# Reordering one step of a chunked linear-attention recurrence: full-array products in one block, scores in quarter tiles

## The chip, the cores and the metric

The kernel runs on one core of a Trainium2 chip, from inputs in device memory to the output in device memory. The metric is the device time of one execution in microseconds; smaller is better. Engines are named as the profile names them: PE is the matrix engine (PEld its weight loads), DVE the vector engine, ACT the scalar engine, POOL GpSimd, SP the queue that issues most DMAs.

## What is computed

Two layers. The first is a recurrence with a decaying state per batch and head; the second sends each resulting row to one of 16 experts, chosen by a group gate and then an expert gate, and multiplies the expert's output by both gates.

```python
# r, k, v: (4 batches, 8 heads, 768 tokens, 48); w, u: (8, 48)
for t in range(S):
    cur = einsum('bhd,bhe->bhde', u * k_t, v_t)
    y[:, :, t] = einsum('bhd,bhde->bhe', r_t, state + cur)
    state = w * state + einsum('bhd,bhe->bhde', k_t, v_t)
x = y reshaped to (3072 tokens, 384)
g_idx = argmax(x @ w_group);  e_idx = argmax(x @ w_expert[g_idx])
out[token] = g_w * e_w * (relu(x @ w1[g, e]) @ w2[g, e])      # w1: 384x1024, w2: 1024x384
```

## The kernel before

All data is f32. The 3072 tokens are 24 tiles of 128: tile n is the chunk n // 4 of batch n % 4. Tiles 2g and 2g+1 are the group g, and are loaded together. The kernel has two stages: a loop of 24 steps (`for s in range(NT)`) for the recurrence and the routing, and then 16 slots, one expert each.

**One step.** The state is replaced by a product of 128x128 per head: the transposed keys and queries, scaled by powers of w, give the scores; the part after the diagonal is kept, and the diagonal holds r*u*k summed over the head. The functions of a step, with the line that issues the work:

- `values(s)` (L505): the scores' matrix `am` times v, 8 heads, 48 output columns each, into the bank pair `YB`.
- `update(s)` (L516): keys times values, 8 heads, 48x48, into `MS`; `carry(s)` (L529, L530, DVE) adds it to the state R. The last four tiles have none.
- `turn(n, "kT")` and `turn(n, "rT")` (L447): four 128x128 transposes each, both into the bank `TR`; kT is copied out by ACT (L456), rT by DVE with a factor (L458). They work at tile s+3.
- `rows_out(s-1)` (L550, and ACT L554): y back to rows, four transposes into `RW`.
- `scores(s+2)` (L465): 8 heads, 48 rows of contraction, 128x128 each, into `PA`; `mask` (L471, DVE) moves the wanted part to `am`.
- `diagonal(n, e)` (L483, ACT): per head one copy of the identity times the head's sum, in two blocks of four; `sum_own(n)` (L438, DVE) makes those sums from `own` (L421, L423, POOL). `scaled` (L431, POOL) makes the scaled keys that kT is made from. POOL does whole groups (two tiles in one instruction), at even and odd steps.
- `gate_parts(s)` (L540): four products of 32 output columns, into `MS`, copied by ACT to `lT` (L545); `gate_sum(s)` (L564) sums them, into another part of `MS`.
- `state(s+1)` (L496): the state's share of the next tile's y, 8 heads of 48 rows and 48 output columns, into `YB`.
- In every four steps the routing of four finished tiles: `route_1` (DVE, reads `MS`), `route_2`, the prefix products `route_p` (L176, L179), `route_3`, `route_4`, and `route_5` (L215, POOL), which scatters rows to their expert's region `x_sorted`.

**What sets the order.** The schedule is manual: every engine runs its instructions in the order in which the program calls the functions, and waits are put in where a buffer or a PSUM bank is still used. A write of PE into a bank waits for the reads of that bank that stand before it in the program, other columns too. On PE a product is two records in the trace (f32 takes two passes with a weight load each), a transpose is one.

**Forms.** Transposes, `gate_sum` and the prefix use the whole 128x128 array. The values and the update use halves of its columns, the scores halves of its rows, `gate_parts` quarters of its columns, the state quarters (half the rows, half the columns).

Of the kernel before, what the change touches and what calls it, by code (L numbers as in the profile page):

```python
# [13 lines left out]
OP = mybir.AluOpType  # L14
# [13 lines left out]
def kernel(  # L28
# [194 lines left out]
    with ExitStack() as rec:  # L223
# [13 lines left out]
        y_ps = YB[:, :, 0 : 2 * P]  # L237

# [58 lines left out]
        for a in range(2):  # L297
            load_half(raw[0, "k"], k, 0, a, both[a])
            load_half(raw[0, "r"], r, 0, a, both[1 - a])
        zeros = ring.tile([P, XW], FP32, name="zeros")  # L300
# [4 lines left out]
        nc.scalar.dma_start(  # L305
            out=ub.rearrange("p h d -> p (h d)"), in_=bass.AP(tensor=u.tensor, offset=u.offset, ap=[[0, P], [1, H * D]])
        )
# [106 lines left out]
        def own(g, half=None, part=None):  # L414
            rt, kt = raw[g, "r"], raw[g, "k"]
            if g not in dgs:
                dgs[g] = pool.tile([P, 2, H, D], FP32, tag="dg", bufs=3, name="dg")
            dg = dgs[g]
            if half is None:
                if part in (None, 0):  # L420
                    nc.gpsimd.tensor_mul(dg, rt, kt)  # L421
                if part in (None, 1):
                    nc.gpsimd.tensor_mul(dg, dg, spread(ub, 1, 2))  # L423
            else:
                nc.gpsimd.tensor_mul(dg[:, half], rt[:, half], kt[:, half])
                nc.gpsimd.tensor_mul(dg[:, half], dg[:, half], ub)

        def scaled(g, half=None):
            dst = kp[g % NKP][:, :, :, 0:D]
            if half is None:  # L430
                nc.gpsimd.tensor_mul(dst, raw[g, "k"], spread(T2, 1, 2))  # L431
            else:
                nc.gpsimd.tensor_mul(dst[:, half], raw[g, "k"][:, half], T2)
# [8 lines left out]
        def turn(n, name, bank=None, early=False):  # L442
            ps = turned[n, name] = TR if bank is None else bank
            src = (kp if name == "kT" else rp)[(n // 2) % NKP]
            for hc in range(HC):
                two = src[:, n % 2, 2 * hc : 2 * hc + 2, :].rearrange("p e x -> p (e x)")
                nc.tensor.transpose(ps[:, hc, :], two, ident)  # L447
# [3 lines left out]
        def turn_out(n, name):  # L451
# [3 lines left out]
            if name == "kT":  # L455
                nc.scalar.copy(dst, ps)  # L456
            else:
                nc.vector.tensor_tensor(out=dst, in0=ps, in1=pw, op=OP.mult)  # L458

        def scores(n):  # L460
            kT, rT = rkT.pop((n, "kT")), rkT[n, "rT"]
            for hc in range(HC):
                for e in range(2):
                    rows = slice(DP * e, DP * e + D)
                    nc.tensor.matmul(  # L465
                        PA[:, e, P * hc : P * (hc + 1)], lhsT=kT[rows, hc, :], rhs=rT[rows, hc, :],
                        start=True, stop=True, skip_group_check=True,
                    )
# [11 lines left out]
        def diagonal(n, e):  # L480
            du = dus[n].rearrange("p (hc e) -> p e hc", e=2)
            for hc in range(HC):
# [53 lines left out]
        def gate_parts(n):  # L536
            yT = yTs[n]
            for q in range(NQ):
                e, j = q // 2, q % 2
                nc.tensor.matmul(  # L540
                    MS[32 * q : 32 * (q + 1), 0:P], lhsT=gwp[:, 4 * j + e, :], rhs=yT[:, e, j, :],
# [3 lines left out]
            nc.scalar.copy(lT, MS[:, 0:P])  # L545
# [157 lines left out]
        scaled(2)  # L703
        same = ring.tile([P, HC], FP32, name="same")
        LA = 3
        late = []
        left = []
        for s in range(NT):
# [9 lines left out]
            if s % 2 == 0 and g < NG:  # L718
                if g > 2:
                    scaled(g)  # L720
                own(g, None, 0)
            if s % 2 == 1 and g < NG:
                own(g, None, 1)
            for c, i in late[0 : 1 if s < 22 else 2]:
                route_5(c, (i,))
            del late[0 : 1 if s < 22 else 2]
# [8 lines left out]
            if s in (1, 2, 3, 4):  # L735
                fill(s - 1)
            far = s + LA < NT
            values(s)
            update(s)
            values_out(s)  # L740
            for c in range(NB - 1):
                if s == 4 * c + 5:
                    route_e(c)
            carry(s)
# [459 lines left out]
```

## Time and profile before

| | us |
|---|---|
| median of 3 runs | 444.2 (442.93 to 445.17) |
| the profiled execution | 445.16 |
| its span, first to last instruction | 443.4 |
| PE busy in the span | 396.9 (90%) |
| first `values` of step 0 / step 4 / step 20 / step 23 starts at | 17.7 / 48.7 / 138.2 / 151.8 |
| first product of the expert stage starts at | 171.8 |

All times below are from the profiled execution and count from the first instruction. A row of a timeline has the start, the length, the engine, the line, the operation, output <- inputs, rows*columns, the shape and the count of merged records. Ends of matmul records are modelled and overlap, so this document reads PE by the distance from one block's start to the next block's start. Square brackets hold the idle time ahead of a row and what released it.

### The profile page before, as it was taken

How to read it: one execution, taken by the hardware profiler on the slowest of the kernel's cores; microseconds unless marked ns; L12 is line 12 of the kernel's file. 1: busy time of each engine (PE TensorE's matmuls, PEld its weight loads, DVE VectorE, ACT ScalarE, POOL GpSimd, SP SyncE). 2: the span in 40 equal slices, each digit the busy share in tenths (PEclk: the TensorE clock that was granted, in tenths of full speed). 3: DMA queues.
4: the chain of work that ended last, by engine and by line, in shares of the span. 5: the costliest groups of instructions: out<-in, count | busy, mean ns of one | idle time of the engine just before them, and what ended most of it. 6: DMA issues, size and time to landing. Idle time of an engine off the chain costs nothing.

```text
span 443.4 us, 9627 instructions
## 1 busy us (share of the span) xinstructions
PE 396.9 (90%) x3506; PEld 371.5 (84%) x3506; DVE 150.9 (34%) x389; ACT 192.6 (43%) x461; POOL 203.1 (46%) x240
## 2 busy tenths in 40 slices
PE   3787999999999825999999999999999999999980
PEld 2666787878788614999999999999999999999970
DVE  6456676767776362020220220220220122022110
ACT  3358777777777303234243244243244334423410
POOL 6689536666643331023614524524523633452435
PEclk9999999999999955999999999999999999999995
DMA  9899997731996627397798898899998999999000
GB/s 151 118 192 215 189 184 149 148 84 38 197 270 174 213 85 168 76 250 167 226 267 180 233 273 178 237 256 208 245 275 178 251 266 214 252 259 258 21 23 25
DMA packets 122902, 81.97 MB, mean 185 GB/s; under 512 B 96420, under 2 KB 114020, under 8 KB 122848
## 3 DMA queue, kind: packets, MB, share of 16 engines
q1 hardware_dynamic: 114976, 70.98, 70.6%
q0 software_dynamic: 4960, 9.55, 7.7%
q10 hardware_dynamic: 2912, 0.77, 1.0%
q8 instruction: 29, 0.48, 0.5%
q14 instruction: 25, 0.20, 0.2%
HBM read 70.09 MB, written 11.68 MB: 184 GB/s over the span
## 4 chain that ended last, share of the span: by engine, by line
issue 45%; PE 26%; POOL 16%; DVE 4%; DMA 4%; ACT 3%; POOLq 1%; DVEq 0%; ACTq 0%
POOL out_dram L900 16%; PE TR L447 6%; PE YB L505 5%; PE PA L465 5%; DMA out_dram<-yt,idn 3%; PE YB L496 3%; PE MS L540 2%; ACT am L483 2%; PE MS L516 2%; PE RW L550 1%; PE MS L564 1%; POOL x_sorted L215 1%; DVE du L438 1%; DMA x_sorted<-xt,place_i 1%; DMA wraw<-in_w_dram 0%
## 5 line engine op out<-in xcount | busy, mean ns | idle before, releaser
L900 POOL DMA_INDIRECT out_dram<-yt,idn x107 | 103.9, 971 | 167.4 <-DVE yt L898 125.4
L876 PE MATMUL ph<-xe,w 128*128 128x200 f32 (+12 forms) x768 | 133.2, 334 | 8.1 <-DMA w<-in_moe_w_dram 8.1
L876 PEld LDWEIGHTS ph<-xe,w 128*128 128x128 f32 x768 | 130.3, 193 | 8.7 <-issue 8.1
L888 PE MATMUL po<-hT,w2p 128*128 128x200 f32 (+12 forms) x768 | 130.4, 330 | 0.0
L888 PEld LDWEIGHTS po<-hT,w2p 128*128 128x128 f32 x768 | 128.1, 190 | 0.0
L897 DVE STREAM_TRANSPOSE yt<-yT 128x672 f32<-128x672 f32 (+1 forms) x16 | 13.6, 847 | 211.1 <-ACT yT L891 211.1
L881 ACT ACTIVATE hT<-ph 128x416 f32<-128x416 f32 (+12 forms) x64 | 31.9, 498 | 101.9 <-PE ph L876 100.4
L483 ACT ACTIVATE am<-ident,du 128x128 f32<-128x128 f32 x184 | 58.6, 397 | 7.6 <-DVE du L438 7.6
L866 ACT COPY w2p<-w 128x1024 f32<-128x1024 f32 x48 | 47.0, 1046 | 11.9 <-POOL yT L823 11.9
L215 POOL DMA_INDIRECT x_sorted<-xt,place_i x24 | 24.0, 998 | 50.4 <-issue 43.9
L891 ACT COPY yT<-po 128x208 f32<-128x208 f32 (+12 forms) x48 | 15.5, 323 | 69.2 <-PE po L888 67.3
L471 DVE COPY_PREDICATED am<-later,PA 128x1024 f32<-128x1024 int32 x24 | 31.3, 1304 | 13.3 <-PE PA L465 7.6
L465 PE MATMUL PA<-rT,kT 48*128 48x128 f32 x384 | 30.6, 304 | 0.0
L505 PE MATMUL YB<-am,vt 128*48 128x128 f32 x384 | 26.8, 283 | 3.2 <-DVE am L471 3.2
L465 PEld LDWEIGHTS PA<-rT,kT 48*128 48x128 f32 x384 | 25.7, 204 | 4.3 <-issue 3.7
L505 PEld LDWEIGHTS YB<-am,vt 128*48 128x48 f32 x384 | 20.5, 125 | 7.4 <-DVE am L471 3.6
L534 ACT COPY yT<-YB 128x512 f32<-128x512 f32 x24 | 14.0, 584 | 28.0 <-PE YB L505 28.0
L431 POOL TENSOR_TENSOR kp<-kt,T 128x768 f32<-128x768 f32 x10 | 18.3, 1830 | 9.1 <-PE MS L516 4.6
L456 ACT COPY kT<-TR 128x512 f32<-128x512 f32 x24 | 14.0, 583 | 12.5 <-PE TR L447 12.0
L421 POOL TENSOR_TENSOR dg<-rp,kt 128x768 f32<-128x768 f32 x10 | 18.3, 1826 | 1.0 <-DMA rp<-in_r_dram 1.0
L423 POOL TENSOR_TENSOR dg<-dg,ub 128x768 f32<-128x768 f32 x10 | 18.3, 1827 | 0.4
L447 PE MATMUL TR<-ident,kp 128*128 128x128 f32 x96 | 17.6, 311 | 0.9 <-DVE rT L458 0.9
(140 smaller groups left out, 317.9 us busy)
## 6 DMA issues: line engine op xcount, KB each, us to landing
w<-in_moe_w_dram SPq DMA_DIRECT2D x128, 384.0 KB, 8.5
vt<-in_v_dram SPq DMA_DIRECT2D x24, 192.0 KB, 5.2
kt<-in_k_dram SPq DMA_DIRECT2D x23, 192.0 KB, 4.6
rp<-in_r_dram SPq DMA_DIRECT2D x23, 192.0 KB, 5.2
xg<-x_sorted SPq DMA_DIRECT2D x42, 85.8 KB, 4.7
out_dram<-yt,idn POOLq DMA_INDIRECT x107, 4.9
x_sorted<-zeros SPq DMA_DIRECT2D x4, 392.0 KB, 5.0
xg<-x_sorted SPq DMA_DIRECT2D x20, 73.5 KB, 5.1
```

The lines of the kernel that those rows point to most:

```text
L215: ins = nc.gpsimd.indirect_dma_start(out=xs_dram, out_offset=bass.IndirectOffsetOnAxis(ap=place_i[:, i : i + 1], axis=0), in_=xt[:, i].rea ...
L421: nc.gpsimd.tensor_mul(dg, rt, kt)
L447: nc.tensor.transpose(ps[:, hc, :], two, ident)
L465: nc.tensor.matmul(PA[:, e, P * hc : P * (hc + 1)], lhsT=kT[rows, hc, :], rhs=rT[rows, hc, :], start=True, stop=True, skip_group_check=True,)
L471: nc.vector.copy_predicated(am[n % NAM], later.unsqueeze(1).unsqueeze(1).to_broadcast([P, 2, HC, P]).bitcast(I32), PA.rearrange("p e (h t) ...
L483: nc.scalar.mul(am[n % NAM][:, e, hc, :], ident, du[:, e, hc : hc + 1])
L505: nc.tensor.matmul(y_at(e, hc), lhsT=vt[:, n % 2, 2 * hc + e, :], rhs=amn[:, e, hc, :], start=(n < 4 and hc < 2), stop=True, skip_group_ch ...
L866: nc.scalar.copy(o4[:, kk], v4[:, kk])
L876: nc.tensor.matmul(ph[:, i, 0:n], lhsT=w1[:, ko, P * (f + i) : P * (f + i + 1)], rhs=xe[:, ko].rearrange("p i b -> p (i b)")[:, 0:n], star ...
L881: nc.scalar.activation(hTs[s][:, f : f + 2, 0:n], ph[:, :, 0:n], AF.Relu)
L888: nc.tensor.matmul(po[:, 0:n], lhsT=w2p[:, d, fo, :], rhs=hT[:, fo, 0:n], start=(fo == 0), stop=(fo == FO - 1))
L900: ins = nc.gpsimd.indirect_dma_start(out=out_q, out_offset=bass.IndirectOffsetOnAxis(ap=idn[:, i : i + 1].bitcast(U32), axis=0), in_=yt[:, ...
```

## The change

Ten edits, all in the recurrence:

- In a step PE now runs values, update, kT, rows_out, rT, gate_sum, (prefix), gate_parts, scores, state. `gate_sum` is that of the tile before, the prefix stands a step later.
- rT goes to the free columns of `YB` (`RT`), and `gate_parts` to `TR` (`lT_ps`), not to `MS`.
- `scores` issues two products per head in place of one: keys 0 to 63 against all 128 queries, keys 64 to 127 against queries 64 to 127, in the two column halves. Tile 0 keeps the old form.
- The lookahead of the transposes is 2 tiles in steps 0 to 2 and 3 after that; step 2 makes two tiles ready. Scores work one tile ahead up to step 2, then two; step 3 does two.
- `own` and `scaled` are done per tile: six instructions on half the elements where three stood for a group.
- `sum_own` runs four tiles ahead, at the step's end.
- The first diagonal block is split into two pairs around the rows' copy; the second stands at the step's end.
- Before the loop, `sum_own(0)` and tile 0's diagonal stand ahead of tile 1's transposes; the load of `u` is issued before the second half of k.
- The zeros for `x_sorted` are written from steps 4 to 7, not 1 to 4.
- The last scatters of step 23 are four, those of step 22 one.

The diff, cut to its core:

```diff
+        RT = YB[:, :, 2 * P : 4 * P].rearrange("p b (h t) -> p b h t", t=P)
+        lT_ps = TR[:, 0, :]
...
+        def own(g, a):
...
+            nc.gpsimd.tensor_mul(dg, raw[g, "r"][:, a], raw[g, "k"][:, a])
+            nc.gpsimd.tensor_mul(dg, dg, ub)
+
+        def scaled(g, a):
+            nc.gpsimd.tensor_mul(kp[g % NKP][:, a, :, 0:D], raw[g, "k"][:, a], T2)
...
-            ps = turned[n, name] = TR if bank is None else bank
+            ps = (TR if name == "kT" else RT) if bank is None else bank
...
+                    for z in range(2):
+                        nc.tensor.matmul(
+                            PA[64 * z : 64 * (z + 1), e, P * hc + 64 * z : P * (hc + 1)],
+                            lhsT=kT[rows, hc, 64 * z : 64 * (z + 1)], rhs=rT[rows, hc, 64 * z : P],
+                            start=True, stop=True, skip_group_check=True,
+                        )
...
-                    MS[32 * q : 32 * (q + 1), 0:P], lhsT=gwp[:, 4 * j + e, :], rhs=yT[:, e, j, :],
+                    lT_ps[32 * q : 32 * (q + 1), :], lhsT=gwp[:, 4 * j + e, :], rhs=yT[:, e, j, :],
...
-        turn(1, "rT", YB[:, 0].rearrange("p (h t) -> p h t", t=P))
         sum_own(0)
         diagonal_here(0)
+        diagonal(0, 1)
+        turn(1, "rT", YB[:, 0].rearrange("p (h t) -> p h t", t=P))
         scores(0)
         turn(1, "kT")
-        diagonal(0, 1)
         mask(0)
...
+            if g < NG:
+                own(g, s % 2)
+                scaled(g, s % 2)
...
+            far = s + (3 if s > 2 else 2)
+            whole = s > 2 and far < NT
+            if far < NT:
+                turn(far, "kT")
+            if whole:
+                diagonal(far, 0, 0, 2)
             if s >= 1:
                 rows_out(s - 1)
+            if whole:
+                diagonal(far, 0, 2, HC)
...
+            if far < NT:
+                turn(far, "rT")
+            if s >= 1:
+                gate_sum(s - 1)
+            for c in range(NB - 1):
+                if s == 4 * c + 6:
+                    route_p(c)
...
+            gate_parts(s)
...
+            ahead = s + (2 if s > 2 else 1)
+            if 0 < s and ahead < NT:
+                scores(ahead)
+                mask(ahead)
             if s + 1 < NT:
                 state(s + 1)
...
+            if whole:
+                diagonal(far, 1)
+            if s >= 2 and s + 4 < NT:
+                sum_own(s + 4)
```

Where it moves instructions, three places. First, PE in step 15 and the first rows of step 16. TR and RW are banks of whole-array transposes, YB the bank pair of y, PA the scores, MS the bank of update, gate and prefix. Before:

```order
L505 MATMUL YB<-am_115,vt 48x128 x8
L516 MATMUL MS<-vt,kp_107 48x48 x8
L447 MATMUL TR<-ident,kp_105 128x128 x4
L550 MATMUL RW<-ident,yT 128x128 x4
L465 MATMUL PA<-rT,kT 128x128 x8
L540 MATMUL MS<-yT,gwp 32x128 x4
L447 MATMUL TR<-ident,rp_109 128x128 x4
L564 MATMUL MS<-sel,lT 128x20
L496 MATMUL YB<-rT,R_100 48x128 x8
L505 MATMUL YB<-am_112,vt 48x128 x8
```

The whole-array blocks stand in two places of the step, and six of its nine blocks are followed by one of another form. After, step 16 (the pair of scores rows stands eight times):

```order
L513 MATMUL YB<-am_112,vt 48x128 x8
L524 MATMUL MS<-vt,kp_104 48x48 x8
L442 MATMUL TR<-ident,kp_105 128x128 x4
L558 MATMUL RW<-ident,yT 128x128 x4
L442 MATMUL YB<-ident,rp_109 128x128 x4
L572 MATMUL MS<-sel,lT 128x20
L548 MATMUL TR<-yT,gwp 32x128 x4
L472 MATMUL PA<-rT,kT 64x128
L472 MATMUL PA<-rT,kT 64x64
...
L504 MATMUL YB<-rT,R_101 48x128 x8
```

Four whole-array blocks now follow each other, the scores have the state's form, and four blocks are followed by another form.

Second, ACT in step 3, which later steps repeat with other buffers: yT is the copy of y, kT and xt the copies out of TR and RW, lT the gate's, am the diagonal. Before:

```order
L534 COPY yT<-YB 128x512
L456 COPY kT<-TR 128x512
L554 COPY xt<-RW 128x2x4x48
L483 ACTIVATE am_114<-ident,du 128x128 x4
L545 COPY lT<-MS 128x128
L483 ACTIVATE am_114<-ident,du 128x128 x4
```

After:

```order
L542 COPY yT<-YB 128x512
L451 COPY kT<-TR 128x512
L491 ACTIVATE am_114<-ident,du 128x128 x2
L562 COPY xt<-RW 128x2x4x48
L491 ACTIVATE am_114<-ident,du 128x128 x2
L553 COPY lT<-TR 128x128
L491 ACTIVATE am_114<-ident,du 128x128 x4
```

The work is the same; two diagonal copies moved ahead of the rows' copy. Third, ACT before the loop, where am_112 is tile 0's matrix and T_76 a table of factors. Before:

```order
L456 COPY kT<-TR 128x512
L687 COPY T_76<-RW 128x384
L456 COPY kT<-TR 128x512
L483 ACTIVATE am_112<-ident,du 128x128 x4
L534 COPY yT<-YB 128x512
```

After:

```order
L451 COPY kT<-TR 128x512
L695 COPY T_76<-RW 128x384
L491 ACTIVATE am_112<-ident,du 128x128 x4
L451 COPY kT<-TR 128x512
L491 ACTIVATE am_113<-ident,du 128x128 x4
```

Tile 0's diagonal moved ahead of tile 1's copy, and tile 1's ahead of the first copy of y.

## Rows read from the trace of the kernel before

**Rows 1.** Windows by stage: busy time (records) of each engine, granted clock, DMA share, GB/s.

```profile
17.70:48.71 31.01, 26.68 (x317) 21.89 (x317) 17.66 (x26) 19.68 (x60) 24.80 (x44) 1.00 1.22 198
48.71:138.24 89.53, 87.05 (x1399) 72.81 (x1395) 63.63 (x166) 66.43 (x201) 49.38 (x43) 1.00 0.71 151
...
171.80:432.00 260.20, 258.55 (x1536) 257.74 (x1536) 42.42 (x93) 88.40 (x157) 98.12 (x101) 0.99 0.83 208
```

**Rows 2.** Timeline of PE, step 15 whole, to the start of step 16.

```profile
110.72 1.08 PE L505 MATMUL YB<-am,vt 128*48 128x128 f32 x16
111.63 0.53 PE L516 MATMUL MS<-vt,kp 128*48 128x48 f32 x16
112.09 0.66 PE L447 MATMUL TR<-ident,kp 128*128 128x128 f32 x4
112.58 0.60 PE L550 MATMUL RW<-ident,yT 128*128 128x128 f32 x4
113.11 1.16 PE L465 MATMUL PA<-rT,kT 48*128 48x128 f32 x16
114.20 0.43 PE L540 MATMUL MS<-yT,gwp 128*32 128x128 f32 x8
114.56 0.66 PE L447 MATMUL TR<-ident,rp 128*128 128x128 f32 x4
115.12 0.40 PE L564 MATMUL MS<-sel,lT 128*128 128x20 f32 x2
115.45 0.66 PE L496 MATMUL YB<-rT,R 48*48 48x128 f32 x16
116.04 1.08 PE L505 MATMUL YB<-am,vt 128*48 128x128 f32 x16
```

**Rows 3.** Timeline of PE in windows of 10 ns: records then under way, from the first.

```profile
112.91 0.27 PE L550 MATMUL RW<-ident,yT 128*128 128x128 f32 x1
113.11 0.38 PE L465 MATMUL PA<-rT,kT 48*128 48x128 f32 x2
...
113.32 0.50 PE L465 MATMUL PA<-rT,kT 48*128 48x128 f32 x6
...
115.71 0.40 PE L496 MATMUL YB<-rT,R 48*48 48x128 f32 x8
...
115.82 0.29 PE L496 MATMUL YB<-rT,R 48*48 48x128 f32 x4
```

**Rows 4.** Waits of PE, 48.7 to 155 us: total, times, longest.

```profile
PE MS L540 <- DVE ex L197: 2.1, 4, 0.6
...
PE MS L540 <- DVE keys L609: 0.4, 1, 0.4
```

**Rows 5.** Timeline of DVE in step 15: the mask of tile 17.

```profile
114.39 1.31 DVE L471 COPY_PREDICATED am<-later,PA 128x1024 f32<-128x1024 int32 x1 [0.51 <-PE PA L465]
```

**Rows 6.** POOL by line and form, whole run: busy us, mean ns.

```profile
L431 POOL TENSOR_TENSOR kp<-kt,T 128x768 f32<-128x768 f32 x10 | 18.3, 1830 | 9.1 <-PE MS L516 4.6 <-DMA kt<-in_k_dram 4.3
...
L425 POOL TENSOR_TENSOR dg<-rp,kt 128x384 f32<-128x384 f32 x4 | 4.0, 1002 | 0.0
```

**Rows 7.** Timelines of PE, ACT and DVE ahead of step 0.

```profile
11.39 2.08 PE L465 MATMUL PA<-rT,kT 48*128 48x128 f32 x16
...
17.70 1.95 PE L505 MATMUL YB<-am,vt 128*48 128x128 f32 x16 [3.19 <-DVE am L471]
...
14.55 0.58 ACT L456 COPY kT<-TR 128x512 f32<-128x512 f32 x1 [2.94 <-PE TR L447]
15.03 1.27 ACT L483 ACTIVATE am<-ident,du 128x128 f32<-128x128 f32 x4
...
16.34 1.31 DVE L471 COPY_PREDICATED am<-later,PA 128x1024 f32<-128x1024 int32 x1 [2.93 <-ACT am L483]
```

**Rows 8.** Timeline of PE in the last steps: prefix, gate sum, values of step 23.

```profile
146.85 0.43 PE L176 MATMUL MS<-ohe,later 128*128 128x64 f32 x2 [0.44 <-ACT lT L545]
...
147.35 0.35 PE L564 MATMUL MS<-sel,lT 128*128 128x20 f32 x2
...
151.76 1.08 PE L505 MATMUL YB<-am,vt 128*48 128x128 f32 x16
```

More of the change, by code (lines that the diff above doesn't have):

```diff
@@ L478, in diagonal_here, with diagonal @@
             nc.vector.copy_predicated(am[n % NAM][:, 0], spread(id_ps, 1, HC).bitcast(I32), spread(du[:, 0], 2, P))
-        def diagonal(n, e):
+        def diagonal(n, e, first=0, last=HC):
             du = dus[n].rearrange("p (hc e) -> p e hc", e=2)
-            for hc in range(HC):
+            for hc in range(first, last):
                 nc.scalar.mul(am[n % NAM][:, e, hc, :], ident, du[:, e, hc : hc + 1])
@@ L717 @@
             del left[0 : 1 if s < 18 else 2]
[L718 to L724, printed above, removed]
+            if g < NG:
+                own(g, s % 2)
+                scaled(g, s % 2)
+            for c, i in late[0 : 1 if s < NT - 1 else 4]:
                 route_5(c, (i,))
-            del late[0 : 1 if s < 22 else 2]
+            del late[0 : 1 if s < NT - 1 else 4]
             if s == 0:
@@ L734, with own_term @@
                 last_consts()
[L735 to L744, printed above, removed]
+            if s in (4, 5, 6, 7):
+                fill(s - 4)
+            def own_term(n):
+                sum_own(n)
+                diagonal(n, 0)
+                diagonal(n, 1)
             if s == 0:
@@ L748 @@
                 diagonal(1, 1)
+            values(s)
+            update(s)
+            values_out(s)
+            carry(s)
+            if s == 0:
                 scores(1)
                 mask(1)
-                turn(2, "kT")
-                turn(2, "rT")
-                sum_own(2)
-                diagonal(2, 0)
-                diagonal(2, 1)
-            begun = s >= 2
-            if far:
-                turn(s + LA, "kT")
-                if begun:
-                    sum_own(s + LA)
+            if s == 3:
+                scores(4)
+                mask(4)
+            far = s + (3 if s > 2 else 2)
[4 more added lines that the diff above has]
+                diagonal(far, 0, 0, 2)
             if s >= 1:
                 rows_out(s - 1)
+            if whole:
+                diagonal(far, 0, 2, HC)
             for c in range(NB - 1):
-                last = c == NB - 2
+                if s == 4 * c + 5:
+                    route_e(c)
+            if far < NT:
[5 more added lines that the diff above has]
+                    route_p(c)
+                    if c == 2:
+                        count(12)
+            gate_parts(s)
+            for c in range(NB - 1):
                 if s == 4 * c + 4:
@@ L772 @@
                         choose_two()
-                if s == 4 * c + (6 if last else 7):
+                if s == 4 * c + (6 if c == NB - 2 else 7):
                     route_4(c)
```

76 lines of the change are left out of this document (29 added, 47 removed).

## The prediction

> **What bounds the kernel now.** I read the windows by stage first, then PE's timeline of one step, then PE's waits, and last who releases the blocks ahead of step 0. The expert stage has PE busy 258.55 of 260.20 us [rows 1], and the change touches nothing in it, so whatever the recurrence gives or takes goes straight to the end. In the middle of the recurrence, steps 4 to 19, PE is busy 87.05 of 89.53 us, while DVE has 63.63, ACT 66.43 and POOL 49.38 [rows 1]: PE sets the pace, 89.53 / 16 = 5.60 us a step, of which 4.15 are busy on ACT and 3.98 on DVE. That DVE waits for PE and not the other way round is seen at the mask, which stands idle 0.51 for the scores [rows 5].
>
> A step in which PE waits for nobody takes 5.32 us (110.72 to 116.04). By the distances of the starts it is: values 0.91, update 0.46, kT 0.49, rows 0.53, scores 1.09, gate parts 0.36, rT 0.56, gate sum 0.33, state 0.59 [rows 2]. Part of this is not products. The four transposes of the rows start 0.11 apart (112.58 to 112.91 [rows 2, 3]), so four cost 0.44; the block took 0.53, because the first scores come 0.20 after the last transpose. The scores' second pair then starts 0.21 after the first, where the sixteen records in 1.09 make 0.11 a pair [rows 2, 3]. Every change of form thus costs about 0.1 us on either side of it, and a step has six. Besides, PE waits 2.1 us at four steps for the routing's last read of the bank that `gate_parts` writes, and 0.4 at one step for the choice of experts [rows 4].
>
> **The change part by part**, in us against the profiled execution.
>
> *The block.* Four whole-array blocks follow each other. The rows lose their change: 0.53 to 0.44, so 0.09. rT loses one on either side: 0.56 to 0.44, so 0.12. Gate sum, gate parts, values, update and kT keep what they have.
>
> *Scores in quarters.* The records double to 32, in quads of two with 128 columns and two with 64. The trace has no such mix. The nearest row is the state, the same quarters with 128 columns each: its quads start 0.11 apart (115.71, 115.82 [rows 3]). With eight quads, each as long as its wide member, that is 8 x 0.11 = 0.88, and 0.03 for the first load: the state's fourth quad starts 0.37 after its first (115.45 to 115.82 [rows 2, 3]), 0.04 over three times 0.11. So 0.91 in place of 1.09: 0.18. The wide products alone fill their quarter for 0.88, so there is no further gain below this; above, quads may run as pairs: half of 16 x 0.11 + 16 x 0.055 is 1.32, or 0.41 more. I take 0.91, by the state's row. The state then follows in its own form: 0.59 to 0.53, so 0.06.
>
> Sum: 0.09 + 0.12 + 0.18 + 0.06 = 0.45 a step, 5.32 to 4.87. Over 16 steps 7.2.
>
> *The banks.* `gate_parts` goes to the bank of kT, which the routing doesn't read. The 2.1 + 0.4 = 2.5 of waits [rows 4] fall away. What is late next is the copy of kT, which now holds that bank: PE has rows, rT and gate sum (0.44 + 0.44 + 0.33) between kT and the gate parts, and the copy is a 0.58 row [rows 7] that starts behind the copy of y, so it is covered. If ACT were a microsecond late, each step would pay the excess. rT shares the bank pair of y: its transposes now wait for the copy of y, which has update and two transpose blocks (1.39) to run in; the state waits for DVE's read of rT, with gate sum, gate parts and scores (1.60) ahead of it. Both covered. Gate sum now waits for the carry's read, which follows the update at once. I cost these waits at nothing; the bound is rival B.
>
> *POOL.* Per step 1.5 instructions of 1.83 become 3 of 1.00 [rows 6]: 2.75 to 3.00, so 0.25 more on 49.38 / 16 = 3.09 [rows 1]. At 3.34 of 4.87 POOL stays off the path; behind it queue the scatters, which have a step each.
>
> *Early sums, split diagonals.* The number of instructions is the same. They keep ACT's and DVE's queues fed ahead of PE: at 4.15 and 3.98 busy in 4.87 both have about 0.7 left. Cost nothing, again up to rival B.
>
> Steps 4 to 19: 7.2 + 2.5 = 9.7.
>
> *Steps 20 to 22.* Before they take 151.76 - 138.24 = 13.52 [rows 1, 8]. After: step 20 lacks the update, 4.87 - 0.46 + 0.09 for the change that then follows the values = 4.50. Step 21 has values 1.00, rows 0.49, gate sum 0.33, gate parts 0.36, scores 0.91, state 0.53 = 3.62. Step 22 the same without scores, with the prefix (147.35 - 146.85 = 0.50 [rows 8]) = 3.21. Together 11.33, so 2.2 gained; the 0.44 wait of the prefix for the gate's copy [rows 8] is in it.
>
> *Ahead of step 4.* The array runs at half pace here: the values' 16 records last 1.95 at 17.70 and 1.08 in step 15, though the granted clock reads 1.00 throughout [rows 1, 2, 7]. Step 0 waits 3.19 for the mask, the mask 2.93 for the diagonal, and ACT does the diagonal at 15.03 behind kT of tile 1 at 14.55 [rows 7]. With the diagonal ahead of that copy, the mask waits for the scores alone: 11.39 + 2.08 = 13.5, the mask 1.31, and 0.05 for either hand-over (16.34 + 1.31 to 17.70 [rows 7]); values start near 14.9 in place of 17.70: 2.8. From step 0 to 4 the 31.01 us [rows 1] hold PE at 26.68 busy, partly at half pace; the change moves one tile's work from step 0 into step 2, where the eight diagonal copies of each of two tiles stand in one queue. I take 0.2 gained there, and as bounds for the whole part 0 (the queue of ACT eats the start) and 6 (PE reaches full pace some steps sooner).
>
> *The rest.* `u` earlier, zeros later and the scatters' count move DMAs off and onto stretches in which nobody waits for them; nothing.
>
> Total 9.7 + 2.2 + 3.0 = 14.9. The profiled execution would go from 445.16 to 430.3; against the median of 444.2, which lies 1.0 below it, **429.3**.
>
> **The rivals.** *A: the quads don't run four at a time.* Pairs cost 0.41 in each of some 20 steps, 8.2: 437.5. The state's quads speak against it; that two widths are mixed, which no row shows, speaks for it.
>
> *B: another engine takes the bound.* DVE's 3.98 is a mean over steps with much routing and steps with little; if half of the 16 steps keep today's pace, 8 x 0.45 = 3.6 comes back: 432.9; if all do, 436.5. The sums above speak against it, DVE's and ACT's 80 to 85% for it.
>
> *C, the slower side: weight loads stand bare.* The quarters of one half of the rows take 16 loads for eight. The first load of the scores, which nothing hides, costs 0.10 (0.21 against 0.11 [rows 3]). If a load could not be hidden behind a product of the same rows, 16 loads at 0.05 (half as wide) add 0.8 a step, at the full 0.10 1.6; over 20 steps 16 or 32: 445.3 or 461.3. It decides from 14.9 / 20 / 16 = 0.047 a load. Against it: the values use all rows in both column halves, with 16 loads, and take 0.91 with their changes [rows 2], no room for sixteen times 0.05. [...]
>
> *D: it doesn't do what it says.* If the tenths at a change of form belong to the blocks and not to the change, the block and the state keep 0.09 + 0.12 + 0.06 = 0.27 a step: 4.3 back, 433.6.
>
> **How the numbers follow.** Forecast 0.65 (425 to 432, by the bounds of the early part), B 0.14, A 0.08, D 0.05, C 0.08 (0.02 at its lower price, 0.06 above). The predicted time is the forecast's, 429.3. Forecast, B and D hold 0.84, so the range is 425 to 437. A measurement of this kernel can tell 0.5%, about 2.2 us, from no change: faster 0.65 + 0.14 + 0.08 + 0.05 = 0.92, same 0.02, slower 0.06.
>
> **What would show it.** Right: starts of values 4.8 to 4.9 apart in steps without prefix, about 5.4 with it; eight quads of scores 0.11 apart, about 0.91 to the state; rows and rT 0.44 each; no PE wait for the routing's reads; values of step 0 near 15, of step 4 near 45.7, the expert stage's first product near 157 and its 260 us unchanged. Wrong: scores of 1.3 (A) or over 1.6 (C); PE idle for `lT`, kT or rT in most steps (B); 0.5 still between transposes and the next block of the same form (D); or an expert stage that starts sooner but ends no sooner.

## The result and the profile after

The changed kernel takes **432.07 us** (430.37 to 432.78, 4 runs) against 444.69 (442.93 to 447.42, 4 runs) for the kernel before, run beside it: a ratio of 0.9705, interval 0.9647 to 0.9763. The forecast was 429.3, the range 425 to 437. The profiled execution is one of 432.07 us; its span is 430.3, 13.1 less than before, where the prediction's sum was 14.9. All ratios below leave out executions of a slower state, two of the four with the gate parts back in MS (the profiled one among them) and one of the four with the relieved first steps, so these two ratios don't follow from the medians.

The windows by stage, in the form of [rows 1], are the steps 0 to 3, 4 to 19 and 20 to 22, the expert stage, and two short stretches of steps 17 and 18.

```profile
14.14:43.38 29.24, 21.28 (x394) 17.82 (x395) 16.09 (x26) 19.67 (x60) 22.92 (x31) 0.96 1.03 149
43.38:127.07 83.69, 81.39 (x1652) 73.36 (x1650) 64.72 (x166) 65.39 (x198) 58.66 (x86) 0.97 0.85 184
127.07:139.82 12.75, 11.58 (x216) 9.45 (x214) 8.38 (x25) 7.62 (x23) 4.42 (x10) 1.00 0.88 241
159.77:430.30 270.53, 257.89 (x1536) 257.24 (x1536) 42.97 (x93) 88.41 (x157) 103.96 (x107) 0.97 0.81 202
112.20:115.10 2.90, 0.75 (x25) 0.60 (x18) 2.73 (x9) 1.67 (x7) 2.67 (x6) 1.00 1.05 243
...
116.30:119.70 3.40, 3.40 (x32) 3.31 (x29) 0.71 (x2) 1.98 (x5) 1.40 (x4) 0.50 1.00 204
```

Beside [rows 1] this gives the account, stage by stage. The last column anticipates the experiment that names the cause (weights from step 20, below).

| stage | forecast gain | changed kernel | weights from step 20 |
|---|---|---|---|
| ahead of step 4 | 3.0 | 48.71 - 43.38 = 5.3 | 4.5 |
| steps 4 to 19 | 9.7 | 89.53 - 83.69 = 5.8 | 10.0 |
| steps 20 to 22 | 2.2 | 13.52 - 12.75 = 0.8 | 2.0 |
| step 23 to the first expert product | 0 | 20.05 - 19.95 = 0.1 | -1.65 |
| expert stage to the end | 0 | 271.6 - 270.5 = 1.1 | 1.0 |
| span | 14.9 | 13.1 | 15.9 |

So the sum came out near by luck, by errors of opposite sign: the early part gave 2.3 more, steps 4 to 22 gave 5.3 less, and the last two stretches gave 1.2 that was not forecast. Of the marks that the prediction set, step 0 (near 15) begins at 14.1, step 4 (near 45.7) at 43.4, and the expert stage (near 157) at 159.8. The early part varies between executions: the kernels whose weights alone are moved, below, have the same program up to step 15, and in them step 4 begins at 44.2 and 44.3.

The loop did not give less because the step is longer. Where nothing disturbs it, a step takes 4.78 (68.37 to 73.15), shorter than the 4.87 forecast. Timeline of PE, step 9 of the changed kernel, to be held against [rows 2]:

```profile
68.37 1.08 PE L513 MATMUL YB<-am,vt 128*48 128x128 f32 x16
...
70.23 0.60 PE L558 MATMUL RW<-ident,yT 128*128 128x128 f32 x4
70.67 0.60 PE L442 MATMUL YB<-ident,rp 128*128 128x128 f32 x4
71.11 0.30 PE L572 MATMUL MS<-sel,lT 128*128 128x20 f32 x2
71.33 0.43 PE L548 MATMUL TR<-yT,gwp 128*32 128x128 f32 x8
71.69 0.99 PE L472 MATMUL PA<-rT,kT 48*64 48x128 f32 x30
72.42 0.31 PE L504 MATMUL YB<-rT,R 48*48 48x128 f32 x2
72.50 0.28 PE L472 MATMUL PA<-rT,kT 48*64 48x128 f32 x2
72.56 0.66 PE L504 MATMUL YB<-rT,R 48*48 48x128 f32 x14
73.15 0.32 PE L513 MATMUL YB<-am,vt 128*48 128x128 f32 x2
```

Rows and rT take 0.44 each, as forecast. Scores and state together take 1.46 (71.69 to 73.15; forecast 0.91 + 0.53), and the state's first records slip in between the last scores. Gate sum takes 0.22 in place of 0.33, which was not forecast: it sums the tile before, whose gate copy has long been made, and its second record starts 0.03 after the first (71.11 to 71.14) in place of 0.13 (115.12 to 115.25).

What is lost in the loop is seen in two places where PE stands still in the middle of a block, on no semaphore. First the waits of PE from 99 to 145 us (total, times, longest), then the timeline of steps 17 and 18:

```profile
PE YB L504 <- issue: 2.2, 1, 2.2
...
PE YB L513 <- issue: 1.2, 1, 1.2
```

```profile
112.38 0.54 PE L504 MATMUL YB<-rT,R 48*48 48x128 f32 x7
115.08 0.43 PE L504 MATMUL YB<-rT,R 48*48 48x128 f32 x7 [2.15 <-issue]
...
117.16 1.12 PE L442 MATMUL TR<-ident,kp 128*128 128x128 f32 x4
118.07 1.06 PE L558 MATMUL RW<-ident,yT 128*128 128x128 f32 x4
118.92 1.00 PE L442 MATMUL YB<-ident,rp 128*128 128x128 f32 x4
```

"issue" is a wait that the profile can't put down to anyone. Behind the first one the granted clock drops: 1.00 while PE stands, then 0.50 from 116.3 to 119.7 (windows above), and the blocks of transposes start 0.91 and 0.85 apart, about twice the 0.49 and 0.44 of step 9. Steps 17 and 18 (108.19 to 122.29) took 14.10 where 4.78 and 5.27 stand for such steps elsewhere: 4.05 lost. The second standstill, 1.2, is in step 22, which takes 4.74 where the last kernel below takes 3.16: 1.6 lost. (The profile models the ends of products, so a listed wait is some 0.4 below what the step loses: 1.17 against 1.6.)

The DMA queues show what came late. First, in the changed kernel (packets, MB, share of 16 engines), the queue that did nearly all the work from 100.5 to 112 us, then the instruction queue q8 from 112 to 112.5 and from 59.5 to 100. The last two rows are q8 over the whole run, of the changed kernel and of the kernel before:

```profile
q1 hardware_dynamic: 6974, 2.04, 95.5%
...
q8 instruction: 1, 0.02, 14.4%
...
q8 instruction: 7, 0.11, 1.3%
...
q8 instruction: 32, 0.52, 0.6%
...
q8 instruction: 29, 0.48, 0.5%
```

The profile calls q8 the instruction queue. Its packets are of 16 KB (0.52 MB in 32), and their number follows PE's instructions: 32 with the quarters (3874 matmul records), 29 without (3506; 29 packets also in the changed kernel with whole scores, below). In the 11.5 us from 100.5 on, where the engines were full (q1 at 95.5%) and three of the early weight pieces of 384 KB were issued besides six loads of 192 KB of v and r, not one came; between 59.5 and 100 seven did, one in 5.8 us. The late one, 12.1 after the last, begins at 112.28, lands 1.15 later, and PE goes on 1.65 after that. The theory to test: **PE ran out of instructions**, because in its new pace it uses them faster, and because the packets queue behind the weights. One sign is the same in all runs: the nine standstills inside steps 17 to 22 that the profiles put down to "issue", here and below, each end 1.4 to 2.0 us after a packet of q8 has landed.

### The profile page after: what moved, and what is told of

It reads as the page before. It is cut to its first block, busy times and chain, and to the rows that moved or that the text cites. A ratio compares the mean times of both kernels' runs of the same rounds, so it can differ in the third digit from the quotient of the medians.

```text
span 430.3 us, 10330 instructions
## 1 busy us (share of the span) xinstructions
PE 382.4 (89%) x3874; PEld 366.1 (85%) x3874; DVE 151.4 (35%) x389; ACT 192.2 (45%) x461; POOL 208.3 (48%) x270
## 4 chain that ended last, share of the span: by engine, by line
issue 44%; PE 24%; POOL 17%; DMA 6%; DVE 4%; ACT 3%; POOLq 1%; DVEq 0%; ACTq 0%
POOL out_dram L916 16%; PE PA L472 5%; PE YB L513 5%; DMA out_dram<-yt,idn 5%; PE TR L442 3%; ACT am L491 2%; PE YB L504 2%; PE YB L442 2%; PE RW L558 2%; PE TR L548 2%; PE MS L524 1%; DVE am L479 1%; PE MS L572 1%; POOL x_sorted L215 1%; DMA x_sorted<-xt,place_i 1%
## 5 line engine op out<-in xcount | busy, mean ns | idle before, releaser
L491 ACT ACTIVATE am<-ident,du 128x128 f32<-128x128 f32 x184 | 60.5, 397 | 6.1 <-DVE du L431 6.0
L422 POOL TENSOR_TENSOR dg<-rp,kt 128x384 f32<-128x384 f32 x24 | 24.2, 1009 | 6.7 <-DMA rp<-in_r_dram 4.7
L472 PE MATMUL PA<-rT,kT 48*64 48x128 f32 (+1 forms) x736 | 25.8, 258 | 0.0
L423 POOL TENSOR_TENSOR dg<-dg,ub 128x384 f32<-128x384 f32 x24 | 24.2, 1007 | 2.0 <-DMA ub<-in_u_dram 0.2
L472 PEld LDWEIGHTS PA<-rT,kT 48*64 48x64 f32 x736 | 20.1, 134 | 4.3 <-issue 4.0
L426 POOL TENSOR_TENSOR kp<-kt,T 128x384 f32<-128x384 f32 x22 | 22.3, 1012 | 2.7 <-DMA kt<-in_k_dram 2.7
L455 DVE TENSOR_TENSOR rT<-YB,pw 128x512 f32<-128x512 f32 x22 | 15.2, 691 | 17.4 <-PE YB L442 14.6
```

The source lines that it names most:

```text
L422: nc.gpsimd.tensor_mul(dg, raw[g, "r"][:, a], raw[g, "k"][:, a])
L423: nc.gpsimd.tensor_mul(dg, dg, ub)
L472: nc.tensor.matmul(PA[64 * z : 64 * (z + 1), e, P * hc + 64 * z : P * (hc + 1)], lhsT=kT[rows, hc, 64 * z : 64 * (z + 1)], rhs=rT[rows, hc ...
L491: nc.scalar.mul(am[n % NAM][:, e, hc, :], ident, du[:, e, hc : hc + 1])
```

## The experiments

The rate of instructions and the traffic of the weights were changed apart from each other: fewer instructions in the changed kernel, less traffic in the changed kernel, more instructions in the kernel before.

**Fewer instructions: whole scores.**

```diff
-                    if n == 0:
+                    if True:
                         nc.tensor.matmul(
                             PA[:, e, P * hc : P * (hc + 1)], lhsT=kT[rows, hc, :], rhs=rT[rows, hc, :],
```

> The changed kernel with one product per head in the scores, as before the change (172 PE instructions a step in place of 204). By the prediction's term for the quarters (0.91 in place of 1.09, and 0.06 at the state) a step without prefix takes 4.78 + 0.24 = about 5.0 us, over some 20 steps 4.9 more. Theory 1 (PE stood still twice, 2.2 us at 112.65 and 1.2 us at 135.23, because its next instructions were not there in time, with 40% more of them per microsecond than before the change): with fewer instructions both standstills go, and the 4 us of half clock behind the first with them (some 2 us), so 5.4 comes back: 431 to 433, the same as the changed kernel. Rival (the standstills have nothing to do with the number of instructions): they stay, and the time is 436 to 438.

Measured: 431.32, ratio to before 0.968 (0.9646 to 0.9715). From 14 us on there is no wait on "issue". Packets are held up as long here, 12.9 us apart from 105.7 to 118.6, but it costs little: step 18 takes 5.99 for the 5.48 of other steps with prefix. A step takes 5.00, 0.22 more. PE's timeline, with 1.09 to the state and 0.59 more to the next values:

```profile
75.70 1.16 PE L466 MATMUL PA<-rT,kT 48*128 48x128 f32 x16
76.79 0.65 PE L504 MATMUL YB<-rT,R 48*48 48x128 f32 x16
77.38 0.32 PE L513 MATMUL YB<-am,vt 128*48 128x128 f32 x2
```

So the size of the quarters' term was right (0.24 forecast, 0.22 measured), and in the change as made it bought nothing: what it saves, the standstills cost. In number of instructions the expectation said 40% more per microsecond; worked out from the windows, products and loads together go from (1399 + 1395) / 89.53 = 31.2 to 41.6 per us without standstill ((1653 + 1651) / 79.50, next run), 33% more.

**Less traffic: weights from step 20.**

```diff
-            for job in left[0 : 1 if s < 18 else 2]:
+            for job in left[0 : 0 if s < 20 else 4]:
                 job()
-            del left[0 : 1 if s < 18 else 2]
+            del left[0 : 0 if s < 20 else 4]
```

> The changed kernel with the early weight pieces of two experts issued four per step from step 20 on, not one or two per step from step 16. Theory 1 (the instruction fetch of PE is held up behind the weights on the DMA engines): the standstill of 2.2 us in step 17 and the half clock behind it are gone, steps 16 to 19 take 4.78 to 5.3 each, 4 us earlier; what follows from step 20 on may stand still more. Rival (the rate of PE's instructions alone brings the standstill): it stays at the same instructions in step 17, within 1 us of 2.2. The expert stage may begin later since its first weights land later; without that the time is 428 by theory 1 and 432 by the rival.

Measured: 429.86, ratio 0.9658 (0.9625 to 0.9691). The windows are steps 17, 18, 4 to 19 and 20 to 22; below them the instruction queue from 100.5 to 112:

```profile
108.88:113.66 4.78, 4.78 (x105) 4.31 (x103) 3.97 (x12) 4.15 (x14) 4.48 (x6) 1.00 0.49 110
113.66:118.92 5.26, 5.26 (x108) 4.76 (x106) 4.61 (x14) 4.69 (x16) 4.37 (x8) 1.00 0.20 73
...
44.21:123.71 79.50, 79.38 (x1653) 71.53 (x1651) 64.63 (x166) 65.34 (x198) 57.38 (x80) 0.99 0.76 164
123.71:135.20 11.49, 11.49 (x216) 9.45 (x214) 8.38 (x25) 7.61 (x23) 4.65 (x16) 1.00 1.05 309
```

```profile
q8 instruction: 2, 0.03, 1.0%
```

With the same PE instructions and the DMA share at 0.49 and 0.20 in place of 1.08 and 1.05, two packets came and the standstill is gone, and with it the half clock (step 22, now with four pieces a step, takes 3.49, 0.3 above the last kernel's). Steps 4 to 19 take 79.50, 10.0 less than before: the prediction's 9.7. Of the 5.5 won in the loop up to step 23, 1.75 go again behind it, where 4.9 MB move in place of 2.5: the later weights stand beside the scatters and the reads of `x_sorted`. Another 0.8 were lost ahead of step 4, where the program is the same: that is the spread between executions, not the edit.

**More instructions in the kernel before: quarters alone.** The edit is the new `scores`, in its old place.

```diff
+                    for z in range(2):
+                        nc.tensor.matmul(
+                            PA[64 * z : 64 * (z + 1), e, P * hc + 64 * z : P * (hc + 1)],
+                            lhsT=kT[rows, hc, 64 * z : 64 * (z + 1)], rhs=rT[rows, hc, 64 * z : P],
```

> The kernel before with the scores in quarters alone, in their old place between the rows' transposes and the gate parts. By the prediction's term the scores take 0.91 in place of 1.09, 0.18 a step; PE then waits as long as before for the routing. Over 22 steps 4.0: 440.7. The state keeps its 0.59, since its neighbours don't change. If weight loads of two quarters of one half of the rows stood bare (rival C), the scores take 1.3 or more and the time goes above 447. With theory 1 on PE's instructions a standstill without any semaphore may appear from step 16 on here as well.

Measured: 445.43, ratio 1.0027 (0.9998 to 1.0056): a miss of 4.7. Timeline of PE:

```profile
114.09 1.10 PE L472 MATMUL PA<-rT,kT 48*64 48x128 f32 x32
115.12 0.42 PE L548 MATMUL MS<-yT,gwp 128*32 128x128 f32 x8
115.47 0.66 PE L447 MATMUL TR<-ident,rp 128*128 128x128 f32 x4
116.10 0.40 PE L572 MATMUL MS<-sel,lT 128*128 128x20 f32 x2
...
129.37 0.40 PE L572 MATMUL MS<-sel,lT 128*128 128x20 f32 x2 [1.48 <-issue]
...
137.12 0.75 PE L513 MATMUL YB<-am,vt 128*48 128x128 f32 x9 [0.88 <-issue]
```

Three things. The scores gain only 0.06 (1.03 to the gate parts in place of 1.09): by comparison with the changed kernel, the other 0.16 (1.09 + 0.59 - 1.46 - 0.06) are there only where the state follows in the same form. Even the 0.06 is lost in the step (5.32 as before), because gate sum then waits longer for its copy (rT to gate sum 0.63; 0.56 in [rows 2]). And standstills on "issue" appear, 1.48 and 0.88, where the kernel before has none; steps 17 and 19 take 1.70 and 1.19 more. The profiled execution, 448.15, is one of the longest of ten (442.64 to 448.35), and its granted clock reads 0.50 from 15.8 to 32.8 us, which the kernel before doesn't show, so how often these standstills come isn't shown. In these runs the rate of instructions and the weights' traffic are each needed: take either away, and the standstill of step 17 is gone.

**The start alone,** in the kernel before; the load of `u` is moved as in the change.

```diff
+        sum_own(0)
+        diagonal_here(0)
+        diagonal(0, 1)
         turn(1, "rT", YB[:, 0].rearrange("p (h t) -> p h t", t=P))
-        sum_own(0)
-        diagonal_here(0)
         scores(0)
         turn(1, "kT")
-        diagonal(0, 1)
```

> The kernel before with the start alone of the change: the own sum and the diagonal of tile 0 ahead of tile 1's transposes, and the load of u ahead of the second half of k. By the prediction the values of step 0 start 2.8 earlier, near 14.9, and the whole gains 2.8 less what the following steps eat: 442 against 444.7. If the start's gain of 3.6 in the changed kernel comes from this edit alone, values start near 14.1. Rival: the queue of ACT in steps 0 to 3 eats it, step 4 begins at 48.7 as before and the time stays at 444.7.

Measured: 440.67, ratio 0.9892 (0.9843 to 0.9941). The values of step 0 and of step 4:

```profile
14.01 1.08 PE L506 MATMUL YB<-am,vt 128*48 128x128 f32 x16 [1.12 <-DVE am L472]
...
44.58 1.08 PE L506 MATMUL YB<-am,vt 128*48 128x128 f32 x16
```

The start gives 3.7 at step 0 (17.70 in [rows 7]) and 4.1 at step 4; the rest of the kernel keeps its pace (steps 4 to 19: 89.5). So ACT's queue does not eat it, and 4.1 come from this edit. The changed kernel has 5.3 ahead of step 4, or 4.4 and 4.5 in the two kernels with the same program up to there, so what all else gives, 0.3 to 1.2, is within the spread. Where the prediction was short: it kept half pace for the scores of tile 0, 2.08 [rows 7]. In both kernels with the new start they take 1.16. Part of this isn't the edit's: with quarters alone, whose program is the old one up to there, they took 1.67, and step 0 began at 16.71 in place of 17.70. When the array comes to full pace is not fixed, though the granted clock reads 1.00 ahead of step 0 in the kernel before (8 to 17.7 us) and in the changed one (8 to 14.14); what decides it stays open.

**The bank of the gate parts.**

```diff
-                    lT_ps[32 * q : 32 * (q + 1), :], lhsT=gwp[:, 4 * j + e, :], rhs=yT[:, e, j, :],
+                    MS[32 * q : 32 * (q + 1), 0:P], lhsT=gwp[:, 4 * j + e, :], rhs=yT[:, e, j, :],
```

> The changed kernel with the gate parts back in MS, the bank that the routing reads; the rest of the order stays. The prediction put 2.5 us on the bank (2.1 + 0.4 of PE's waits for the routing). If the bank is what took these waits away, PE waits for the routing's reads again at four steps and the time is some 2.5 above the changed kernel's: 434.5. Rival: the new order alone took them away, since the routing of a step now starts after that step's gate parts and has nearly a whole step until the next ones; then no such wait is seen, the starts of values stay 4.78 apart, and the time is the changed kernel's 432.

Measured: 433.21, ratio 0.9654 (0.9567 to 0.9741), an interval too wide for 2.5 us; the trace decides. From 46 to 111 us no wait for the routing's reads is listed for the gate parts. But in every fourth step the read isn't free: in step 9 the update, which also writes MS, starts 1.08 after the values (70.21 to 71.29) in place of 0.91, and the step takes 5.07 for 4.78:

```profile
70.21 1.08 PE L513 MATMUL YB<-am,vt 128*48 128x128 f32 x16
71.29 0.56 PE L524 MATMUL MS<-vt,kp 128*48 128x48 f32 x16
...
118.38 0.37 PE L504 MATMUL YB<-rT,R 48*48 48x128 f32 x1 [2.14 <-issue]
```

So the new bank is worth 0.3 to 0.4 in each of four steps (5, 9, 13 and 17), 1.3 in all, about half of the 2.5; the order, which puts the routing's reads behind the gate parts of its step, gave the other half. Step 15 takes 0.51 more besides, its gate sum waiting 0.65 for DVE; whether the bank is behind that isn't shown. The last row shows the standstill of step 17 in the same block as in the changed kernel, at nearly the same length.

**One block taken out: the rows between gate parts and scores.**

```diff
-            if s >= 1:
-                rows_out(s - 1)
             if whole:
                 diagonal(far, 0, 2, HC)
...
+            if s >= 1:
+                rows_out(s - 1)
             ahead = s + (2 if s > 2 else 1)
```

> The changed kernel with the transposes of the rows taken out of the block and put between the gate parts and the scores, as one more change of form. By the prediction a change costs about 0.1 on either side: kT, rT and gate sum still follow each other, but the rows get their 0.53 back in place of 0.44, so a step without prefix takes 4.87 in place of 4.78, 2 us over some 21 steps: 434. Rival D (the tenths belong to the blocks, not to the change): the step stays at 4.78 and the time at 432.

Measured: 435.67, ratio 0.9793 (0.9765 to 0.9822). A step takes 5.11 (72.63 to 77.73). PE's timeline:

```profile
74.92 0.30 PE L572 MATMUL MS<-sel,lT 128*128 128x20 f32 x2
75.33 0.42 PE L548 MATMUL TR<-yT,gwp 128*32 128x128 f32 x8
75.68 0.66 PE L558 MATMUL RW<-ident,yT 128*128 128x128 f32 x4
76.27 0.99 PE L472 MATMUL PA<-rT,kT 48*64 48x128 f32 x30
```

The rows take 0.59 (75.68 to 76.27) outside the block and 0.44 in it: a change of form on both sides costs 0.15, so rival D falls. The other 0.18 were not expected: gate sum to gate parts is 0.41, since the gate parts now come 0.44 sooner after kT and wait for its copy out of the bank that they share. This is the "late next" that the prediction named and costed at nothing, and the rows are the cover that it rested on. With this slower step the 2.2 standstill is gone too (0.7 is left in step 22).

**A better place for the weights, and for the first steps.** Three kernels build on each other. First, three pieces per step from step 18:

```diff
-            for job in left[0 : 1 if s < 18 else 2]:
+            for job in left[0 : 0 if s < 18 else 3]:
```

> The changed kernel with the early weight pieces three per step from step 18 on, so that all sixteen are issued in the loop, none while k, r and v are still loaded, and none behind the loop. By theory 1 the standstill in step 17 and the half clock behind it are gone, the pieces land before the expert stage wants them, and step 23 begins 4 us earlier as with four per step from step 20; the first product of the expert stage waits for the scattered rows alone: 428 to 429. If three per step are enough to hold up PE's instructions, a standstill of 1 to 2 us is seen in steps 19 to 22 and the time is 430 to 431.

Measured: 429.01, ratio 0.9631 (0.9603 to 0.9658). Steps 4 to 19 take 80.2; 0.77 of standstill are left in step 22. Then the first steps:

```diff
+            if s in (1, 2):
+                sum_own(s + 2)
...
+            if s in (1, 2):
+                diagonal(s + 1, 1)
+            if s == 3:
+                diagonal(5, 1)
...
-            if s <= 2:
-                own_term(far)
+            if s == 0:
+                sum_own(2)
+            if s < 2:
+                diagonal(s + 2, 0)
             if s == 2:
                 turn(5, "kT")
                 turn(5, "rT")
-                own_term(5)
+                diagonal_here(4)
+                diagonal(4, 1)
+                sum_own(5)
+                diagonal_here(5)
```

> The kernel with three weight pieces per step from step 18, and besides the first four steps made to wait less for ACT: the second half of a tile's diagonal stands behind the copies of y and kT of the next step, the first half of tiles 4 and 5 is done by DVE, own sums of tiles 3 and 4 stand ahead of the mask, scaled keys ahead of the own products in steps 0 and 1. In the changed kernel steps 1 to 3 take 6.9, 8.0 and 8.7 and PE waits 0.8, 0.3 and 1.7 for the copy of y behind diagonals and 1.45 for rT. If ACT's queue is what makes these steps long, step 4 begins 3 to 4 us earlier, near 40, and the time is 425. Rival: the steps are bound by the loads of k and r and by the half clock, step 4 begins near 43, and the time is that of the weight pieces alone.

Measured: 424.48, ratio 0.9489 (0.9451 to 0.9528). Step 4 begins at 38.42, 5.9 sooner than with the weights alone (44.29). PE's longest wait from 14 to 44 us of the changed kernel, and from 14 to 40 of this one:

```profile
PE YB L442 <- ACT yT L542: 2.7, 3, 1.7
```

```profile
PE YB L513 <- DVE am L479: 2.5, 2, 1.5
```

The 2.7 for the copy of y behind ACT's diagonals are gone. The clock differs too, as the windows of steps 0 to 3 show, first with the weights alone, then here:

```profile
14.63:44.29 29.66, 23.55 (x394) 20.10 (x395) 16.13 (x26) 19.91 (x60) 23.55 (x32) 0.87 0.94 158
14.16:38.42 24.26, 19.55 (x394) 17.02 (x394) 16.34 (x28) 15.60 (x46) 18.95 (x23) 1.00 0.92 139
```

With the weights alone 7.7 us of this stretch stand at half clock, here none. Of the 5.9, that can be up to 3.8 (an estimate: half of the 7.7); whether the shorter waits also kept the clock up isn't shown, so the two aren't told apart. But a standstill came back in step 22, behind the second record of the values:

```profile
126.41 0.42 PE L513 MATMUL YB<-am,vt 128*48 128x128 f32 x2
129.04 1.07 PE L513 MATMUL YB<-am,vt 128*48 128x128 f32 x14 [2.21 <-issue]
```

At this very place PE also stood in the changed kernel (1.17) and with the weights alone (0.77): always the same instruction. So the pieces were given out one at a time, three times in a step, each behind a small write on DVE that keeps them apart:

```diff
-            nc.gpsimd.memset(w1[32 * i : 32 * (i + 1), 0, 0:1] if i < NQ else w2[:, 2 * (i - NQ), 0:1], 0.0)
+            nc.vector.memset(w1[32 * i : 32 * (i + 1), 0, 0:1] if i < NQ else w2[:, 2 * (i - NQ), 0:1], 0.0)
...
             carry(s)
+            piece()
...
+            piece()
             if s >= 1:
                 gate_sum(s - 1)
...
                 mask(ahead)
+            piece()
```

> The kernel with the relieved first steps, and the sixteen early weight pieces given out one at a time, three times in each step from step 18 on, each released by a small write on DVE between the step's other work; with three at the step's start PE still stood 2.2 us in step 22 while its next instructions landed. If it is the backlog on the DMA engines that holds up the fetch, pieces of 384 KB about 1.6 us apart leave it no backlog and no standstill is seen from step 4 on: 2.2 us less, 422 to 423. If it is the bandwidth in use as such, or the number of PE's instructions alone, the standstill of 1 to 2.5 us stays somewhere in steps 18 to 23 and the time is 424.5.

Measured: 423.35, ratio 0.9519 (0.9455 to 0.9583). At the same place 0.20 is left of the wait (step 22 takes 3.77 in place of 5.78, 0.6 above the last kernel's 3.16):

```profile
124.84 0.42 PE L513 MATMUL YB<-am,vt 128*48 128x128 f32 x2
125.47 1.07 PE L513 MATMUL YB<-am,vt 128*48 128x128 f32 x14 [0.20 <-issue]
```

The bandwidth in use doesn't hold the packets up by itself, then (291 GB/s in steps 20 to 22 with three per step, 298 with single ones). That the backlog does is likely but not shown: four pieces at the start of each step from step 20, at 309 GB/s, lost only 0.3 at this place. Of the 2 us gained there the stretch up to the expert stage takes 1.8 back (22.0 from step 23 to its first product, 20.2 at three per step): the last pieces land beside the scatters. The intervals of this kernel and the one before overlap; which of the two is better isn't shown. Last, step 0's gate parts done in step 1:

```diff
-            gate_parts(s)
+            if s != 0:
+                gate_parts(s if s > 1 else 0)
...
                 mask(ahead)
+            if s == 1:
+                gate_parts(1)
             piece()
```

> The same, and the gate parts of step 0 done in step 1, so that PE doesn't wait in step 0 for the gate's weights, whose load is issued at 17.1 us: in the kernel with relieved first steps PE stood 2.2 us there with no semaphore in the profile. If that standstill is the load, the values of step 1 start about 1.4 us earlier (they then wait for rT and the mask, ready at 18.7), and the time is 421.5. If it is PE's instructions (a packet of them lands at about that time), the standstill stays at another product.

Measured: 423.81, ratio 0.9511 (0.9457 to 0.9566). The values of step 1 follow those of step 0 after 4.55 in place of 5.46, and no wait on "issue" is left from 10 us on: the one in step 0 was the load of the gate's weights, not instructions. The 0.9 are lost again by the expert stage, whose first product begins 23.9 after step 23. All three end below both kernels of this study; the gain over the changed kernel is 1.9 to 2.2% by the ratios.

## Why the prediction was right, and where it was not

**The bound** was read rightly. PE sets the pace after the change too: from 46 to 111 us the profile lists no wait of PE, so rival B has nothing to show, though its 432.9 lies nearer the measured time than the forecast does. Rivals A and C fall with the scores: 30 of their 32 records start within 0.73 (71.69 to the state's first at 72.42), and the eighth pair of wide products starts 0.81 after the first (72.50), with no room for sixteen bare loads of 0.05. By the prediction's estimate they would have added 0.8 a step or more; the forecast without them has 1.44 for scores and state, and 1.46 was measured, with 32 loads for the scores of a tile (L472: 736 loads in 23 tiles). One reading in the prediction is loose: sixteen records in 1.09 are 0.14 a pair; 0.11 is the distance of the pairs inside the block, without its ends.

**The block** was forecast at 0.45 a step and gave 0.54 (5.32 to 4.78). The rows' 0.09 and the 0.12 of rT are met, scores and state gave 0.22 for 0.24, and 0.11 came from gate sum. The split of the 0.24 was wrong: quarters alone save 0.06, the rest is the change of form that goes where the state follows.

**The banks** gave their 2.5 but for one delay of 0.4 (gate sum in step 15, which takes 5.19), about half by the order and half by the bank. Steps 4 to 19 without a standstill took 79.5 (9.7 forecast, 10.0 measured), steps 20 to 22 11.2 in the last kernel (2.2 forecast, 2.3 measured).

**The step that failed** is the one that isn't there: the prediction counted the doubled records of the scores as PE time alone and never asked who delivers the instructions. 33% more of them per microsecond, with packets held up behind weights, cost 5.6 us: 4.05 in steps 17 and 18, the half clock included, and 1.6 in step 22. That covers the 5.3 by which steps 4 to 22 fell short. No rival names it; that the total came near is luck, since the start gave more than its term. From step 5 to 16 (46 to 111 us) no "issue" wait stands. With weights on full engines (a DMA share of 1.05 from 112.2 to 115.1, of 1.03 from 135 to 136) there are two: 2.15 and 1.17.

**The start** was sized at 2.8 + 0.2 and gave 5.3. The mechanism was right in the main: the mask of step 0 starts at 12.80 in place of 16.34, though not behind the scores alone, which end at 12.43; the diagonal and DVE's copy of rT end at 12.76. The pace of the array was not right: it came to full pace before the scores of tile 0 (1.16 in place of 2.08), not after step 0. The bounds, 0 to 6, held it. Of the steps 1 to 3 the prediction said that eight diagonal copies of two tiles stand in one ACT queue; that cost was there, 2.7 of waits for the copy of y, and could be taken out.

**The expert stage** was taken as unchanged. It gave 1.1. The half clock that stands at its start lasted 4.3 us into it and 5.7 in the kernel before, which can be 0.7 of it (an estimate: half of the difference); nothing here was tested.

**Costed at nothing and, from step 4 on, rightly so:** POOL by tile, the early sums, the split diagonals, the shared banks; the last of these only because the rows stand between kT and the gate parts. In steps 1 to 3 the bank that rT shares with y cost the 2.7 above.

## What to carry to other kernels

When an edit makes instructions smaller and more (here 33% more per microsecond), count them per microsecond on the engine that sets the pace, and look at which transfers stand beside the instruction queue. The sign here was a standstill inside a block, with "issue" as its only reason and in step 22 always at the same instruction (1.17, 0.77 and 2.21 us). Large loads that have time are better given out one by one than several at the start of a step: here that took a standstill from 2.21 to 0.20, though the whole time didn't clearly gain. And a gain that lies in two neighbours having the same form, as 0.16 of the 0.22 of scores and state did, can't be tested, or costed, one block at a time.

## What the runs showed of the hardware

- In the changed kernel, behind 384 KB pieces on full DMA engines (q1 at 95.5%), an instruction packet of 16 KB came 12.1 us after the one before, where one in 5.8 came from 59.5 to 100 us, and PE went on 1.65 us after it had landed (113.43 to 115.08). In all nine such standstills of steps 17 to 22 PE went on 1.4 to 2.0 us after a landing.
- A standstill of 2.15 us was followed, 1.2 us after PE had resumed, by 3.4 us at a granted clock of 0.50; step 18, which holds them, took 6.85 where such a step takes 5.27. With the weights from step 20 the clock stayed at 1.00 there.
- Quarters of unequal width (128 and 64 columns) run side by side: in step 9 of the changed kernel, behind the first, the pairs of wide products start 0.11 us apart (72.07, 72.18, 72.29), as the state's quads do in the kernel before (115.71, 115.82), and the state's first products (72.42) slip in ahead of the last scores (72.50).
- A change of form cost 0.15 us where a block of four transposes stood between two blocks of other forms (in the kernel with the rows between gate parts and scores: 0.59 in place of 0.44).
- Full pace of the array came at different times ahead of step 0 in programs that are the same up to there (scores of tile 0: 2.08 in the kernel before, 1.67 with quarters alone). In the kernel before the granted clock reads 1.00 from 8 to 17.7 us.
